# Landed keys copied by ScalarE, three raw-weight buffers, and a new hand-written order: a gated linear recurrence followed by a PReLU network on one core

## The chip, the cores and the metric

The kernel runs on one core of one Trainium2 chip. The metric is the device time of one execution in microseconds, lower is better. Five engines work in parallel, each through its own instructions in program order: TensorE (PE; its weight loads are listed as PEld), VectorE (DVE), ScalarE (ACT), GpSimd (POOL) and SyncE (SP), which here only issues DMAs. An instruction that has to wait holds up everything behind it on its engine.

## The reference

Inputs are float32. The first part is a recurrence with a per-channel forget gate, the second a two-layer network on its output.

```python
batch, n_heads, seq, head_dim = (4, 8, 768, 48)
f = 1.0 / (1.0 + np.exp(-f_logit))
for t in range(S):
    state = f[:, :, t, :, None] * state + np.einsum('bhd,bhe->bhde', k[:, :, t], v[:, :, t])
    y[:, :, t] = np.einsum('bhd,bhde->bhe', q[:, :, t], state)
...
n_tokens, d_model, d_ff = (3072, 384, 2048)
x = y.transpose(0, 2, 1, 3).reshape(B * S, H * D)
h = x @ w_in
g = np.maximum(h, 0.0) + alpha * np.minimum(h, 0.0)
return (g @ w_out).astype(np.float32)
```

## The kernel before

The sequence is cut into 6 chunks of 128 positions and the batch into 2 pairs; one pair of one chunk is a step, so there are 12 steps, numbered 0 to 11, named `bp_c` (pair, chunk). The recurrence of a step is worked out as block products; its state is carried in the tiles `vs0` and `vs1`, one for each pair. The network of step n runs while the attention of step n+1 is worked out.

Each stage of a step is a Python generator, cut by `yield` into pieces:

- `P` (`prepare`, 8 pieces): load f, q, k, v (line 279, 288); sigmoid and copies on ScalarE (293 to 296); products on VectorE (307 to 313); scans (340, 341); two further pieces of VectorE products (347 to 357; `k4`, `us`); the keys scaled to the end of the block and, from the second chunk on, transposed by VectorE into `kt` (407 to 415); the queries `q3` (401, 440); ScalarE copies of them into the score tile `A` (453).
- `K` (`keys_moved`): 16 DMAs from `kt` to `ksn`, 8 issued by SP and 8 by GpSimd (463).
- `S`, `T` (`scores` for the two batches of a pair, 4 pieces each): products on PE (569, on the raw keys, then on `k4`), each followed by predicated copies into `ad` on VectorE (578, 588, 604).
- `O` (`carry`): products between halves of a chunk (497), their ScalarE copies into `A` (504), the state increments on PE (532) and the state update `moved(0)` on VectorE (542, 546). In chunk 0 the keys go through PE transposes and ScalarE copies (514, 518) and not through DMAs. In later chunks two small products with an identity (525) read one column of each landed block of `ksn` just before the state increments; all waits for the 16 DMAs stand on these two.
- `Y` (`attend`): `ad` copied into `A` (612), the output products (623), the copy `y` (630), `moved(1)`, and the DMAs that lay `y` out as `xT` (653); in step 0 this layout is done by PE (642, 644).
- `n` (`network`, 13 pieces after step 0): 8 blocks `ph` of hidden units (668), each followed by a ScalarE pass `neg` (673) and two VectorE passes `gate` (675), sums of gates (754), then 7 products of the second layer, `pa` to `pe` (707), with sums on VectorE (711) and stores from SP (683). The products share four PSUM banks in turn. In step 0 the second layer is the plain one, `po` (688).
- `a`, `w` (w_in, 8 pieces each) and `b`, `g` (w_out): a raw piece of weights of 768 KB is loaded by SP (229), ScalarE splits it with two passes (233, 234), VectorE adds the halves (243). The raw pieces go through `RAWS` buffers in turn. `W` derives the sums of w_out (773), `i` is one idle product that writes nothing used (779), `X` hands over PSUM banks.

The order in which PE, VectorE, ScalarE and SP get their instructions is written out by hand: `START` lists pieces up to step 4, `USUAL` is the pattern for every later step, in which a bare letter means step n, `+` means step n+1, and `n` means the network of step n-1. `S:2` means two pieces of S. The words before are in the diff below. GpSimd's own order follows from its program order and is nearly untouched.

Of the kernel before, what the change touches and what calls it, by code (L numbers as in the profile page):

```python
# [21 lines left out]
U = 2  # L22
# [1 line left out]
NC2 = C // CH  # L24
NB = DB // 4
WP = 768
RAWS, LEADS = 5, 4
UP = 2.0 ** 16

BEGUN = 5  # L30
START = (
# [7 lines left out]
)  # L39
USUAL = "S:2 T:2 n:3 P+ n S P+ T S n:3 T n Y n O P+ O P+ O Y n O P+ Y:2 n:2 P+:2 K+ n P+"  # L40

LOOSE = ("a", "w", "b", "g", "W", "i", "X")

def flat(start, usual, steps=12):
    out = []
    for word in start.split():
        key, _, times = word.partition(":")
        out += [(key,) if key in LOOSE else (key[0], int(key[1:]))] * int(times or 1)
    for n in range(BEGUN, steps + 1):
        for word in usual.split():  # L50
            key, _, times = word.partition(":")
            m = n + key.count("+") - (key == "n")
            if m < steps:
                out += [(key[0], m)] * int(times or 1)
    return out

ORDER = flat(START, USUAL)


@with_exitstack  # L60
def kernel(
# [30 lines left out]
    nc = tc.nc  # L92
# [3 lines left out]
    D = DM // H  # L96
# [3 lines left out]
    T = U * C  # L100
    W = U * HP * C
# [70 lines left out]
    for m in range(1, NB):  # L172
        lo = UO[m] + (4 if m == 1 else 0)
        n = NB - m
# [4 lines left out]
    for half in range(2):  # L179
        for m in range(1, NQ):  # L180
            n = NQ - m
# [9 lines left out]
    ident = const.tile([128, 128], F32, tag="ident", name="ident")  # L191
# [65 lines left out]
    def rows(par):  # L257
        return slice(64 * par, 64 * par + D)
# [4 lines left out]
    def halves(cc):  # L263

        return slice(CH * cc, CH * cc + CH), slice(CH * (1 - cc), CH * (1 - cc) + D)
# [191 lines left out]
    def keys_moved(bp, c, x):  # L457
# [7 lines left out]
                    in_=kt[32 * a:32 * (a + 1)].rearrange("p (g b x) -> p g b x", b=NJ, x=32)[:, :, b, 0:n])  # L465
        yield

    def carry(bp, c, x):

        i = f"{bp}_{c}"  # L470
        home = more if (bp, c) == steps[0] else pairs
        off = home[0]
        if not c:
            half = home[1]
            for u in range(U):
                for hp in range(HP):
                    for j in range(NJ):
                        g = (u * HP + hp) * NJ + j
                        o = (u * HP + hp) * 16
                        for par in range(2):  # L480
                            r_ = rows(par)
                            nc.tensor.matmul(half[DB * j:DB * (j + 1), par, o:o + 16], lhsT=x["k16"][r_, g],
                                             rhs=x["q16"][r_, g], start=True, stop=True)
            yield
            for u in range(U):
                o = u * HP * 16
                nc.scalar.copy(ad[:, u, :, :, 16:DB], half[:, :, o:o + HP * 16].rearrange("p r (h t) -> p r h t", h=HP))  # L487
            yield
        q3, ks, kh, f64 = (x[n] for n in ("q3", "ks", "kh", "f64"))
        for u in range(U):  # L490
            for hp in range(HP):
                a = (u * HP + hp) * NC2
                h_ = slice(64 * (hp % 2), 64 * (hp % 2) + 2 * DB)
                o = (u * HP + hp) // 2 * 2 * DB
                for par in range(2):
                    r_ = rows(par)
                    nc.tensor.matmul(off[h_, par, o:o + 2 * DB], lhsT=kh[r_, a:a + 2].rearrange("p c s -> p (c s)"),  # L497
                                     rhs=q3[r_, a:a + 2, 2], start=True, stop=True)
        yield
        for cc in range(NC2):  # L500
            s_ = slice(CH * cc, CH * cc + DB)
            for e in range(2):
                of = off[64 * e + DB * cc:64 * e + DB * (cc + 1), :, 0:U * HP * DB]
                nc.scalar.copy(A[s_].rearrange("p u (r h e) t -> p r u h e t", r=2, e=2)[:, :, :, :, e, CH * cc + DB:CH * (cc + 1)],
                               of.rearrange("p r (u h c t) -> p r u h c t", u=U, h=HP // 2, c=NC2)[:, :, :, :, cc])


        if not c:
            yield
            pk = home[1]  # L510
            for u in range(U):
                for hp in range(HP):
                    a = (u * HP + hp) * NC2
                    nc.tensor.transpose(pk[:, u, hp * 128:(hp + 1) * 128], ks[:, a:a + 2].rearrange("p c s t -> p (c s t)"), ident)
            yield
            ksn = x["ksn"] = work.tile([128, U, HP * 128], F32, tag="ksn", name=f"ksn_{i}", bufs=1)
            for u in range(U):
                nc.scalar.copy(ksn[:, u], pk[:, u])
        yield
        pd = home[1]  # L520
        ksn = x["ksn"]
        if c:
            for par in range(2):
                r_ = slice(64 * par, 64 * par + 64)
                nc.tensor.matmul(pd[r_, par, 508:512], lhsT=ident[r_, r_], rhs=ksn[r_, 0, 0:128:32], start=True, stop=True)  # L525
        for u in range(U):
            for hp in range(HP):
                for cc in range(NC2):
                    for par in range(2):
                        o = (u * HP + hp) * D  # L530
                        s_ = halves(cc)[0]
                        nc.tensor.matmul(pd[rows(par), cc, o:o + D],  # L532
                                         lhsT=ksn[s_, u, hp * 128 + 64 * par:hp * 128 + 64 * par + D],
                                         rhs=vs[bp][s_, cc, u, (2 * hp + par) * D:(2 * hp + par + 1) * D], start=True, stop=True)

        def moved(cc):

            of, to = halves(cc)[1], halves(1 - cc)[1]
            was, then = (vs[bp][p, a, :, 0:DM].rearrange("p u (h e) -> p u h e", e=D)
                         for p, a in ((of, cc), (to, 1 - cc)))  # L540
            if c or cc:
                nc.vector.tensor_tensor(then, was, f64[of].unsqueeze(3).broadcast_to((D, U, H, D)), ALU.mult)
            for par in range(2):
                now = pd[rows(par), cc, 0:U * HP * D].rearrange("p (u h e) -> p u h e", u=U, e=D)
                if c or cc:
                    nc.vector.tensor_tensor(then[:, :, par:H:2], then[:, :, par:H:2], now, ALU.add)
                else:
                    nc.scalar.copy(then[:, :, par:H:2], now)

        x["moved"] = moved  # L550
        yield
        moved(0)
        yield
# [236 lines left out]
    with tc.manual_schedule(engines={mybir.EngineType.PE, mybir.EngineType.DVE, mybir.EngineType.Activation,  # L790
                                     mybir.EngineType.SP}):
        run = {}
        for n, step in enumerate(steps):
            x = {}
            for key, stage_ in zip("POYKn", (prepare, carry, attend, keys_moved, network)):
                run[key, n] = stage_(*step, x)
            run["S", n], run["T", n] = (scores(u, *step, x) for u in range(U))
        for key in ORDER:
            next(run[key] if key in run else pieces[key[0]])
# [55 lines left out]
```

## Time and profile before

| what | value |
|---|---|
| median of 3 runs | 609.65 us (608.31 to 610.66) |
| profiled execution: time | 608.89 us |
| profiled execution: span in the trace | 607.1 us |
| granted TensorE clock, mean | 0.994 |
| PE busy | 583.9 us, 96% |
| VectorE busy | 495.0 us, 82% |
| ScalarE busy | 242.3 us, 40% |
| GpSimd busy | 85.4 us, 14% |
| DMA | 50.36 MB, mean 83 GB/s |

The span runs from the first to the last instruction of the trace; 1.79 us of the execution's time lie around it. PE's busy time is modelled from pipelined products, so a busy PE can still have small gaps between groups. Times inside the trace are counted from the start of the span. A wait is put down to the engine that released it; "issue" is a stretch in which an engine waited for nothing that the trace shows.

### The profile page before, as it was taken

The numbers are of one execution on the slowest core, as the hardware profiler recorded it, in microseconds if no ns is written. First come the engines' busy times: TensorE is split into PE (matmuls) and PEld (weight loads), VectorE is DVE, ScalarE is ACT, GpSimd is POOL, SyncE is SP. The second block draws the span as 40 slices with busy tenths as digits, with TensorE's granted clock in tenths as the row PEclk, the third lists the DMA queues.
The fourth block names the chain that finished last, engine by engine and source line by source line (L and its number), as shares of the span: only waits on it lengthen the run. The fifth ranks groups of instructions, "written<-read, shape, count | busy, mean of one in ns | idle before, by whom it ended". The sixth has DMA issues, their size and how long they took to land.

```text
span 607.1 us, 18178 instructions
## 1 busy us (share of the span) xinstructions
PE 583.9 (96%) x7786; PEld 521.8 (86%) x7786; DVE 495.0 (82%) x998; ACT 242.3 (40%) x419; POOL 85.4 (14%) x162
## 2 busy tenths in 40 slices
PE   4679999999999999999999999999999999999997
PEld 2568767899899899899899899899889899899997
DVE  7889999998997788598888988988988986982351
ACT  4579944424513712341550541542433424322110
POOL 9210014023003003003001201200300300300000
PEclk9979999999999999999999999999999999999999
DMA  8949516123033111402501601601601601201000
GB/s 269 312 148 350 186 37 141 36 77 92 11 94 99 19 27 36 149 2 56 155 2 46 165 3 42 169 3 41 171 1 39 170 4 29 53 2 24 30 1 26
DMA packets 52880, 50.36 MB, mean 83 GB/s; under 512 B 26720, under 2 KB 43360, under 8 KB 52800
## 3 DMA queue, kind: packets, MB, share of 16 engines
q1 hardware_dynamic: 42784, 37.46, 21.2%
q0 software_dynamic: 5504, 9.90, 6.4%
q10 hardware_dynamic: 4512, 1.85, 1.3%
q8 instruction: 61, 1.00, 0.7%
q14 instruction: 19, 0.16, 0.1%
HBM read 36.21 MB, written 4.72 MB: 67 GB/s over the span
## 4 chain that ended last, share of the span: by engine, by line
PE 92%; ACT 1%; issue 1%; DMA 1%; SPq 0%; DVE 0%; ACTq 0%; DVEq 0%
PE ph L668 42%; PE pa L707 10%; PE pc L707 9%; PE pair L569 6%; PE pe L707 5%; PE pd L707 4%; PE pb L707 4%; PE pair L623 4%; PE po L688 3%; PE pair L532 1%; PE pair L497 1%; DMA xT<-y 1%; PE pair L525 1%; PE xt L642 0%; ACT us L334 0%
## 5 line engine op out<-in xcount | busy, mean ns | idle before, releaser
L668 PE MATMUL ph<-xT,w_in_sb 128*128 128x256 f32 x1152 | 255.7, 381 | 0.0
L668 PEld LDWEIGHTS ph<-xT,w_in_sb 128*128 128x128 f32 x1152 | 216.7, 190 | 31.5 <-issue 1.4
L675 DVE SCALAR_TENSOR_TENSOR gate<-neg,om,ph 128x256 f32<-128x256 f32 x192 | 81.9, 479 | 40.0 <-ACT neg L673 39.8
L673 ACT ACTIVATE neg<-ph 128x512 f32<-128x512 f32 x96 | 56.3, 595 | 115.6 <-PE ph L668 76.9
L707 PE MATMUL pa<-w_out_sb,gate 128*128 128x192 f32 x352 | 61.9, 329 | 0.0
L707 PE MATMUL pc<-t,S 128*128 128x192 f32 x352 | 61.6, 328 | 0.0
L707 PEld LDWEIGHTS pa<-w_out_sb,gate 128*128 128x128 f32 x352 | 57.5, 190 | 1.3
L707 PEld LDWEIGHTS pc<-t,S 128*128 128x128 f32 x352 | 57.4, 190 | 0.4
L453 ACT COPY A<-q 48x512 f32<-48x512 f32 x44 | 27.1, 616 | 74.8 <-DVE q L401 74.4
L463 POOL DMA_DIRECT2D ksn<-kt x80 | 46.2, 586 | 73.2 <-DVE kt L415 46.6
L653 POOL DMA_DIRECT2D xT<-y x22 | 11.9, 545 | 302.5 <-ACT y L630 302.4
L588 DVE COPY_PREDICATED ad<-mquad,pair 128x224 f32<-128x224 int32 (+6 forms) x140 | 41.7, 298 | 5.8 <-PE pair L569 1.7
L578 DVE COPY_PREDICATED ad<-mraw,pair 128x256 f32<-128x256 int32 (+1 forms) x96 | 41.1, 452 | 4.3 <-ACT ad L487 1.3
L711 DVE SCALAR_TENSOR_TENSOR Csum<-pc,Csum 128x192 f32<-128x192 f32 x22 | 7.8, 356 | 39.9 <-PE pc L707 39.8
L357 DVE TENSOR_TENSOR us<-us,fs 128x768 f32<-128x768 f32 (+5 forms) x60 | 36.9, 615 | 1.1
L612 ACT COPY A<-ad 32x512 f32<-32x512 f32 x48 | 29.5, 615 | 20.4 <-DVE ad L588 19.8
L754 DVE TENSOR_TENSOR S<-gate 128x512 f32<-128x512 f32 x44 | 30.3, 688 | 0.8
L707 PE MATMUL pe<-w_out_sb,S 128*128 128x192 f32 x176 | 30.5, 327 | 0.0
L707 PE MATMUL pb<-t,gate 128*128 128x192 f32 x176 | 30.4, 326 | 0.0
L707 PE MATMUL pd<-w_out_sb,S 128*128 128x192 f32 x176 | 30.4, 326 | 0.0
L630 ACT COPY y<-pair 128x512 f32<-128x512 f32 x22 | 11.8, 589 | 46.4 <-PE pair L623 45.8
L707 PEld LDWEIGHTS pe<-w_out_sb,S 128*128 128x128 f32 x176 | 28.9, 190 | 0.1
(121 smaller groups left out, 740.6 us busy)
## 6 DMA issues: line engine op xcount, KB each, us to landing
w_out_raw<-in_w_out SPq DMA_DIRECT2D x8, 767.8 KB, 7.2
w_in_raw<-in_w_in SPq DMA_DIRECT2D x8, 767.2 KB, 10.4
out<-o SPq DMA_DIRECT2D x23, 192.0 KB, 2.0
q<-in_qT SPq DMA_DIRECT2D x8, 512.0 KB, 4.7
k<-in_kT SPq DMA_DIRECT2D x8, 512.0 KB, 5.9
f<-in_fT SPq DMA_DIRECT2D x7, 512.0 KB, 3.9
vs<-in_v SPq DMA_DIRECT2D x16, 192.0 KB, 6.4
ksn<-kt SPq DMA_DIRECT2D x80, 32.0 KB, 2.1
```

Source lines behind the costliest of these rows:

```text
L357: nc.vector.tensor_tensor(us[:, :, UO[m]:UO[m] + 4 * n].rearrange("p g (i r) -> p g i r", r=4), us[:, :, skip:skip + 4 * n].rearrange("p g ...
L453: nc.scalar.copy(A[halves(cc)[1], :, par * HP:(par + 1) * HP, CH * cc:CH * (cc + 1)], q3[rows(par)].rearrange("p (u h c) s t -> p u h c (s ...
L463: (nc.gpsimd if a % 2 else nc.sync).dma_start(out=ksn[32 * b:32 * (b + 1)].rearrange("p u (h x) -> p (u h) x", h=HP)[:, :, 32 * a:32 * a + n],
L569: nc.tensor.matmul(to[DB * j:DB * (j + 1), par, hp * step + lo:hp * step + hi], lhsT=keys[r_, g * DB:(g + 1) * DB], rhs=by[r_, g, lo:hi], ...
L578: nc.vector.copy_predicated(adu[:, :, :, d:4], mraw[:, d, :, d:4].bitcast(I32).unsqueeze(1).broadcast_to((128, H, NB, n)), rv[:, :, QO[d]: ...
L588: nc.vector.copy_predicated(ad[:, u, :, :, 4 * m:DB], mquad[:, lo:lo + n].bitcast(I32).unsqueeze(1).unsqueeze(1).broadcast_to((128, 2, HP, ...
L612: nc.scalar.copy(A[s_].rearrange("p u h t -> p (u h) t")[:, :, s_], ad[s_].rearrange("p u r h t -> p (u r h) t"))
L668: nc.tensor.matmul(ph[:, j * T:(j + 1) * T], lhsT=w_in_sb[:, kt, m * 128:(m + 1) * 128], rhs=xT[:, kt], start=(kt == 0 and j == 0), stop=( ...
L673: nc.scalar.activation(neg, phv, AF.Relu, scale=-1.0)
L675: nc.vector.scalar_tensor_tensor(gate[:, m % NH, m // NH], neg[:, j], om[:, m:m + 1], phv[:, j], ALU.mult, ALU.add)
L707: nc.tensor.matmul(to[:, 0:DH], lhsT=of(f), rhs=by(f), start=(f == 0 and not more), stop=(f == NH - 1), skip_group_check=True)
L754: nc.vector.tensor_tensor(to, x_, y_, op)
```

## The change

Three things change.

1. The two identity products of line 525 go. A new stage `M` (`landed`) takes their place: one ScalarE instruction copies the 48 used columns of each block of `ksn` back into the tile `kt`, and the state increments read `kt`. The wait for the 16 DMAs stands on this copy.
2. `RAWS` goes from 5 to 3.
3. `START` and `USUAL` are replaced. `START` now begins with the first piece of w_in (load, split, add), ahead of the loads of step 0. In `USUAL`, `K` moves to the end of the step, behind the last store of the network; `M` stands behind the fifth network piece; the four pieces of `O` stand together.

Lines of the code after `keys_moved` are numbered 7 higher in the changed kernel up to line 519, and 3 higher from line 526 on.

```diff
-RAWS, LEADS = 5, 4
+RAWS, LEADS = 3, 4
 START = (
-    "i P0:3 S0 i P0:2 T0 i O0:2 a i P0:2 P1 i T0 i:3 O0 T0 O0 P1 S0 P1 S0 O0 T0 S0 i w P0 i P1 O0 P1 O0 i "
-    "Y0:2 O0 a S1 Y0 O1 Y0 O1 X a S1 w Y0 T1 P2 T1 w a:2 w P1 n0 a:2 P1 w a w S1 P2 S1 n0 T1 w P1 w b "
...
+    "a i w P0:3 S0 P0:2 O0 a O0 i:2 P0:2 i T0 a S0 T0 i O0 P0 P1:2 S0 T0 S0 P1 O0 T0 w O0 a i:2 O0 P1 i:2 "
+    "Y0 O0 i:2 S1 Y0 O0 P1 Y0:2 w O1:2 a S1 X Y0 a T1 P2 w T1 n0 w S1 w P1 T1 a P2 S1 a P1 n0 T1 b n0:2 "
...
-USUAL = "S:2 T:2 n:3 P+ n S P+ T S n:3 T n Y n O P+ O P+ O Y n O P+ Y:2 n:2 P+:2 K+ n P+"
+USUAL = "S T S T n:4 P+ M n T S T P+ S P+ n:2 Y n Y O:4 n:2 Y P+:2 Y n:2 P+:2 n P+ K+"
...
+    def landed(bp, c, x):
+        parts = "p u (g x) -> p (u g) x"
+        kn = x["kt"].rearrange("p (u y) -> p u y", u=U)
+        nc.scalar.copy(kn.rearrange(parts, x=64)[:, :, 0:D], x["ksn"].rearrange(parts, x=64)[:, :, 0:D])
+        x["ksn"] = kn
+        yield
...
-        if c:
-            for par in range(2):
-                r_ = slice(64 * par, 64 * par + 64)
-                nc.tensor.matmul(pd[r_, par, 508:512], lhsT=ident[r_, r_], rhs=ksn[r_, 0, 0:128:32], start=True, stop=True)
...
-            for key, stage_ in zip("POYKn", (prepare, carry, attend, keys_moved, network)):
+            for key, stage_ in zip("POYKMn", (prepare, carry, attend, keys_moved, landed, network)):
```

10 rows, old and new, of the table START are left out of this document.

## The prediction

> **What bounds the kernel now.** I read the busy totals, the slices and the chain's shares first. The two rows marked PE are its share in the totals and its busy tenths in 40 slices; the last line is the chain that ended last.
>
> ```profile
> PE 583.9 (96%) x7786; PEld 521.8 (86%) x7786; DVE 495.0 (82%) x998; ACT 242.3 (40%) x419; POOL 85.4 (14%) x162
> ...
> PE   4679999999999999999999999999999999999997
> ...
> PE 92%; ACT 1%; issue 1%; DMA 1%; SPq 0%; DVE 0%; ACTq 0%; DVEq 0%
> ```
>
> From slice 4 on (45 us) PE never stops; the table of windows gives it 46.92 us of the 47.12 us of a late step. So the time is: when PE's unbroken run begins (first network block, 45.16 us), plus PE's own work, plus any wait that the new order puts into it. Second, the chain in order of time (start, length, what) round the two products that go:
>
> ```profile
> 403.46 2.60 PE pb L707 x16
> 406.06 0.62 PE pair L497 x32
> 406.85 0.20 issue
> 407.05 0.19 PE pair L525
> 407.24 0.81 PE pair L532 x62
> 408.05 2.80 PE pc L707 x16
> ```
>
> L497 ends at 406.68, L532 begins at 407.24: line 525 with its waits costs PE 0.56 us. Third, the timeline of the start, rows of ScalarE and PE:
>
> ```profile
> 1.68 1.28 ACT L293 ACT_TABLE_LOAD   x1 [1.68 <-PEq L847]
> ...
> 4.43 0.63 ACT L293 ACTIVATE f<-f 128x512 f32<-128x512 f32 x1 [0.15 <-DMA f<-in_fT]
> ...
> 19.89 0.90 ACT L234 ACTIVATE w_in_sb<-w_in_raw 128x768 int32<-128x768 uint32 x1
> ...
> 27.96 1.25 ACT L453 COPY A<-q 48x512 f32<-48x512 f32 x2
> ...
> 31.49 1.07 ACT L518 COPY ksn<-more 128x512 f32<-128x512 f32 x2
> ...
> 36.50 2.09 PE L623 MATMUL more<-A,vs 128*64 128x64 f32 x64
> ```
>
> The sigmoid waits for f, then ScalarE runs without a gap from 23.8 to 37.7 us, and PE waits 5 us for L518.
>
> **Line 525 gone.** The chain shows the gap of 0.56 us in eight of the ten steps that have it, and 0.21 us in two (126.35 to 126.57, 158.50 to 158.71), where L525 follows longer blocks. 8 x 0.56 + 2 x 0.21 = 4.9 us off PE, if L532 finds its keys ready. All PE products from the first network block on are otherwise the same set in another order.
>
> **The copy M.** No row has 128x768 float32 on ScalarE as a copy; L234 writes 128x768 in 0.91 us, L453 48x512 in 0.62, L296 128x1024 in 1.05. I take 0.85, and 0.3 for sixteen semaphores (17 ns apiece in the waits of L463), 1.15 us in all. ScalarE is 40% busy, so its time is hidden; what counts is when it may run and who stands behind it. In a late step, from the start of the raw-key products (376.43 in the trace) as zero:
>
> ```profile
> 378.04 5.37 SPq L463 DMA_DIRECT2D ksn<-kt  x8
> ...
> 383.23 0.36 DVE L711 SCALAR_TENSOR_TENSOR o<-pe,o 128x192 f32<-128x192 f32 x1
> ...
> 383.66 0.40 SPq L683 DMA_DIRECT2D out<-o  x1
> ...
> 388.62 0.60 ACT L673 ACTIVATE neg<-ph 128x512 f32<-128x512 f32 x1 [0.19 <-PE ph L668]
> 389.24 1.06 ACT L293 ACTIVATE f<-f 128x1024 f32<-128x1024 f32 x1
> ```
>
> K now stands behind that store on SP, so its eight issues run from 7.6 to 13.0 and not from 1.6; the last lands 2.0 us (median of L463) after its issue at 12.4, at about 14.5 to 15.0. The fourth `neg` ends at 12.7, M ends near 16.2, the fifth `neg` (block ready at 14.7) near 16.8. Behind it on VectorE: fifth gate to 17.65, both predicated copies (2 x 2.2) to 22.0, the seven products from L307 on (3.6, now ahead of gates 5 to 7) to 25.7, gates to 28.1; `pa` begins at 25.9 on PE and wants the last gate's first half after 2.4 us, at 28.3; that half is done at 27.7. So PE does not wait, with 0.5 us to spare. Also queued behind K: the loads of f, q, k and v, 384.10 before and some 5 us later now. f lands near 17.5 (3.9 us, median), the sigmoid follows, and its user L307 comes at 22. Hidden. The same walk for the bank of the fifth block (gate 0 done at 11.3, wanted at 12.1) leaves 0.8 us.
>
> **The start.** Raw piece 0 goes ahead of f on SP. 767 KB at the 314 to 335 GB/s of the windows from 2 to 6 us are 2.3 us; f lands at 6.1 and 6.9, not 3.6 and 4.4. ScalarE splits the piece first (5.3 to 7.0: 1.7 from 19.09 to 20.79). The changed program holds a second table load between this and the sigmoid: 1.28 by the row, to 8.3. The second half's sigmoid starts at 8.95, 4.5 us late. The Trainium skill (ScalarE: Activation LUTs, "What ACT_TABLE_LOAD costs") counts a switch at 2.66 us, with a drain of 1.38 beside the load; the trace's one load agrees on 1.28 and shows no drain, since ScalarE waited for f there. By the page the sum below would be 1.4 us higher.
>
> Of the 4.5 us, 1.5 vanish in the wait of VectorE for GpSimd (12.2 to 13.68); `q3` is done at 23.3 and not 20.4. From there ScalarE's work up to the output products, by the trace's start-to-start times: L453 1.28, L293 to L296 2.60, L504 1.52, one raw piece 1.75, L518 0.96, L334 and L336 2.25, L612 2.53, L548 0.96, 13.85 in all: 37.15. Before, the output products began at 36.57. Gone from this stretch are PE's ten idle products at 18.6 to 23.0, which L497 had waited behind, and one raw split. So the first network block begins 0.6 us later, 45.8. Bounds: if nothing were hidden, the whole 4.5; if the ScalarE chain started with `q3` as early as before, -2.3.
>
> **Three buffers.** Piece n may load when n-3 is split, not n-5. By ScalarE's new order raw splits end at 7, 16, 22, 30, 44, 47, 51, 55 us and for w_out from 57.5 to 83.4; each load (7.2 us median) is issued three splits ahead and lands before its turn, the tightest (last piece: issued 73.8, turn at 81.6) by 0.6 us. PE wants its last piece at 93. Hidden.
>
> **The new order between 45 and 235 us.** VectorE is busy 14.5 of 15 us in these windows, so order matters. Walking its new list with the durations above: `q3` of step 1 is done at 57.5 (PE wants it at 58.3), the last gate of the next network at 122.0 (124.0), `moved(0)` of step 2 at 126.5 (the output products, now right behind `pb`, want it at 126.9). No wait, but 0.4 to 2 us to spare where my walk may be 1 us off. Bounds: 0 to 3 us; I take 0, the side on which all three fall.
>
> **Sum.** 608.89 us + 0.6 - 4.9 = 604.6. That execution lies 0.76 under the median of the runs; I put half of this back: 605.0.
>
> **Rivals.**
> 1. *The copy comes late, slower.* M waits for the last of 128-byte pieces, and ScalarE, then VectorE, then `pa` wait behind it. For: only 0.5 us to spare, K now 6 us later, and L463 landings up to 4.8 us. Against: the long landings need heavy traffic, and the loads come behind K in the queue. It decides when the last landing takes over 2.5 us. At 4.0, PE waits 1.5 us in each of eight steps: 605.0 + 12 = 617; at 3.2, 610.6. I put it at 614.
> 2. *The start eats the gain.* f, the table switch and the ScalarE chain hide nothing: first network block 4.5 us later, 609. For: ScalarE has no gap from 23.8 to 37.7. Against: 1.5 us of VectorE's wait are certain cover.
> 3. *The change does not do what it says on PE.* The 0.56 us are not the waits but the turn from one kind of product to another, and L532 pays them anyway, or VectorE's ties take them: 608.5 to 609.5. For: 0.2 of it is "issue". Against: at 76.2 us L532 follows L569 without a gap.
>
> **How the numbers follow.** Forecast 0.55, rival 1 0.15, rival 2 0.17, rival 3 0.13. About 0.5% (3.05 us) is what a measurement can tell from no change: under 606.6 is faster, over 612.7 slower. The forecast gives 0.52 of faster (its own range 602.3 to 607), rivals 2 and 3 another 0.04; they and the upper edge of the forecast give 0.28 of same; rival 1 most of slower. The range 602.3 to 612 leaves out 0.05 below (ScalarE's chain earlier) and 0.12 above.
>
> **What would show it.** In the profile of the changed kernel: two table loads, the second near 7 us, and the first L293 near 8.3; the output products of step 0 (L623 before) near 37.2; the first `ph` at 45.8; late steps 46.56 us long, L532's rows 0.0 us behind L497's; `M` ending before the fifth `neg` is 2.5 us old; no wait of `pa` for a gate. Wrong it is if a late step is 47.1 or longer, or the first `ph` is later than 48.

## The result, and the profile after

The changed kernel takes 614.35 us (611.93 to 631.0, 8 runs), the kernel before 609.63 us (8 runs): the ratio is 1.0073, 95% interval 1.0048 to 1.0098. The forecast was 605.0 with a range up to 612.0; the change makes the kernel about 4.5 us slower. The first profile of the changed kernel caught a disturbed execution (631.0 us), so the one read here is a later one, of 613.87 us with a span of 612.1 (`e1` below).

The busy totals, PE's slices and the chain's shares of the changed kernel:

```profile
PE 582.0 (95%) x7746; PEld 519.7 (85%) x7746; DVE 494.6 (81%) x998; ACT 248.2 (41%) x430; POOL 80.4 (13%) x162
...
PE   0598999999999989999999999999999999999997
...
PE 59%; DVE 2%; issue 0%; DVEq 0%
```

PE still bounds the kernel, with 2 us less work. (The chain of this profile can be followed back only to 235 us, so its 59% stands for PE in the last 61% of the span.) PE's slices are 15.3 us each. The first has fallen from 4 to 0 and the second from 6 to 5, the third has risen from 7 to 9, and two new places stand under 9: the fourth (46 to 61 us, where the first network block now starts) and the fifteenth (214 to 230 us). The late steps are not among them. Here is the chain of the changed kernel round the place of the two products that went (start, length, what):

```profile
408.80 0.62 PE pair L504 x32
409.42 0.72 PE pair L535 x64
410.14 2.80 PE pa L710 x16
```

L504 (L497 before) ends at 409.42 and L535 (L532 before) begins at 409.42. The gap of 0.56 us is gone, and a late step takes 46.39 us (L535 of one step starts at 362.85 in PE's timeline, which shows products that overlap a little earlier than the chain does, and that of the next at 409.24), against 47.12.

The start is where the time went. The timeline of ScalarE in the changed kernel (start, length, line, operation; in brackets what it waited for):

```profile
1.65 1.28 ACT L233 ACT_TABLE_LOAD   x1 [1.65 <-PEq L850]
7.00 0.88 ACT L233 ACTIVATE w_in_lead<-w_in_raw 128x768 f16<-128x768 bf16 x1 [4.07 <-DMA w_in_raw<-in_w_in]
...
8.69 1.28 ACT L293 ACT_TABLE_LOAD   x1
9.98 1.15 ACT L293 ACTIVATE f<-f 128x512 f32<-128x512 f32 x2
...
28.47 1.06 ACT L293 ACTIVATE f<-f 128x1024 f32<-128x1024 f32 x1 [2.14 <-DMA f<-in_fT]
...
32.07 1.49 ACT L511 COPY A<-more 32x256 f32<-32x256 f32 x4 [0.92 <-PE more L504]
...
36.50 1.07 ACT L525 COPY ksn<-more 128x512 f32<-128x512 f32 x2 [1.21 <-PE more L521]
```

The same line before, and ScalarE's one wait in this stretch before:

```profile
3.64 0.63 ACT L293 ACTIVATE f<-f 128x512 f32<-128x512 f32 x1 [0.68 <-DMA f<-in_fT]
...
23.84 1.49 ACT L504 COPY A<-more 32x256 f32<-32x256 f32 x4 [3.05 <-PE more L497]
```

The first sigmoid starts at 9.98 us (3.64 before). After `q3`, ScalarE before waited once, 3.05 us for the products of L497, and then ran without a gap up to the output products. Now it waits three times: for f of step 1, for L504, and for L521. PE's timeline of the changed kernel in the same stretch tells why:

```profile
23.93 0.75 PE L572 MATMUL pair<-qd,k 48*32 48x80 f32 x22
28.76 1.03 PE L572 MATMUL pair<-qd,k 48*32 48x80 f32 x42 [4.07 <-issue]
...
34.50 1.97 PE L521 MATMUL more<-ident,ks 128*128 128x128 f32 x8
...
43.09 1.97 PE L626 MATMUL more<-A,vs 128*64 128x64 f32 x60 [0.76 <-ACT vs L551]
...
47.95 0.41 PE L489 MATMUL pair<-us 48*32 48x16 f32 x34 [1.98 <-issue]
48.28 4.54 PE L645 MATMUL xt<-y,dense 128*128 128x256 f32 x12
...
53.60 2.64 PE L671 MATMUL ph<-xT,w_in_sb 128*128 128x256 f32 x11
```

And before:

```profile
25.63 1.09 PE L514 MATMUL more<-ident,ks 128*128 128x128 f32 x8
...
41.12 0.41 PE L482 MATMUL pair<-us 48*32 48x16 f32 x34 [1.63 <-issue]
41.45 2.86 PE L642 MATMUL xt<-y,dense 128*128 128x256 f32 x12
...
45.09 2.86 PE L668 MATMUL ph<-xT,w_in_sb 128*128 128x256 f32 x12
```

In the middle of one group of products PE stands still for 4.07 us and waits for nothing that the trace shows. After that L521 takes 1.97 us (1.09 before) and `xt` 4.54 (2.86): the granted clock in the table of windows is 0.50 from 30 to 38 and from 50 to 52 us. The output products come at 43.09 (36.50 before), the first network block at 53.60 (45.09).

The other new place is in step 4 (PE's timeline, then ScalarE's, of the changed kernel):

```profile
213.31 0.94 PE L535 MATMUL pair<-vs,kt 64*48 64x48 f32 x64 [0.47 <-ACT kt L471]
...
224.38 0.59 PE L710 MATMUL pa<-w_out_sb,gate 128*128 128x192 f32 x2 [0.19 <-DVE gate L678]
226.47 0.59 PE L710 MATMUL pa<-w_out_sb,gate 128*128 128x192 f32 x2 [1.49 <-DVE gate L678]
...
246.57 13.22 PE L671 MATMUL ph<-xT,w_in_sb 128*128 128x256 f32 x60 [0.17 <-DVE Csum L714]
```

```profile
202.50 0.60 ACT L676 ACTIVATE neg<-ph 128x512 f32<-128x512 f32 x1 [1.99 <-PE ph L671]
212.43 0.83 ACT L471 COPY kt<-ksn 128x768 f32<-128x768 f32 x1 [9.33 <-DMA ksn<-kt]
213.17 1.08 ACT L676 ACTIVATE neg<-ph 128x512 f32<-128x512 f32 x2
```

ScalarE stands 9.33 us in the copy of step 4, because SP issues that step's `K` only from 204.86 on, behind a store, and the copy stands right behind it. The next two `neg` passes (L676) queue behind the copy, VectorE's gates come late, and `pa` waits. PE loses 0.47 + 0.19 + 1.49 + 0.17 = 2.3 us.

So the account of the two profiled executions is: start +8.5 us (45.09 to 53.60); all that follows −3.5 us (span minus first block: 562.0 before, 558.5 after), which is +2.3 in step 4 and, as the remainder, −5.8 saved; in sum +5.0, from 608.89 to 613.87.

### The profile page after: what moved, and what is told of

It reads as the page before. It is cut to its first block, busy times and chain, and to the rows that moved or that the text cites. A ratio compares the mean times of both kernels' runs of the same rounds, so it can differ in the third digit from the quotient of the medians.

```text
span 629.2 us, 18037 instructions
## 1 busy us (share of the span) xinstructions
PE 600.4 (95%) x7746; PEld 530.4 (84%) x7746; DVE 494.9 (79%) x998; ACT 249.4 (40%) x430; POOL 80.4 (13%) x162
## 4 chain that ended last, share of the span: by engine, by line
PE 91%; DVE 3%; ACT 2%; issue 2%; DMA 1%; SPq 1%; ACTq 0%; DVEq 0%
PE ph L671 39%; PE pa L710 10%; PE pc L710 9%; PE pair L572 6%; PE pe L710 5%; PE pd L710 5%; PE pb L710 5%; PE pair L626 4%; PE po L691 4%; PE pair L535 1%; PE pair L504 1%; DMA w_in_raw<-in_w_in 1%; PE xt L645 1%; SPq L463 1%; PE more L782 1%
## 5 line engine op out<-in xcount | busy, mean ns | idle before, releaser
L671 PE MATMUL ph<-xT,w_in_sb 128*128 128x256 f32 x1152 | 265.3, 392 | 0.0
L671 PEld LDWEIGHTS ph<-xT,w_in_sb 128*128 128x128 f32 x1152 | 220.0, 193 | 38.0 <-issue 1.5
L676 ACT ACTIVATE neg<-ph 128x512 f32<-128x512 f32 x96 | 56.2, 595 | 123.0 <-PE ph L671 95.2
L710 PE MATMUL pa<-w_out_sb,gate 128*128 128x192 f32 x352 | 64.9, 339 | 1.1 <-DVE gate L678 1.1
L710 PE MATMUL pc<-t,S 128*128 128x192 f32 x352 | 63.2, 335 | 0.0
L710 PEld LDWEIGHTS pc<-t,S 128*128 128x128 f32 x352 | 59.8, 192 | 0.1
L572 PE MATMUL pair<-qd,k 48*32 48x80 f32 x1536 | 21.2, 244 | 15.5 <-ACT us L334 11.9
L572 PEld LDWEIGHTS pair<-qd,k 48*32 48x32 f32 x1536 | 17.9, 109 | 20.9 <-ACT us L334 12.6
L710 PE MATMUL pe<-w_out_sb,S 128*128 128x192 f32 x176 | 31.8, 336 | 0.0
```

The source lines that it names most:

```text
L572: nc.tensor.matmul(to[DB * j:DB * (j + 1), par, hp * step + lo:hp * step + hi], lhsT=keys[r_, g * DB:(g + 1) * DB], rhs=by[r_, g, lo:hi], ...
L671: nc.tensor.matmul(ph[:, j * T:(j + 1) * T], lhsT=w_in_sb[:, kt, m * 128:(m + 1) * 128], rhs=xT[:, kt], start=(kt == 0 and j == 0), stop=( ...
L676: nc.scalar.activation(neg, phv, AF.Relu, scale=-1.0)
L710: nc.tensor.matmul(to[:, 0:DH], lhsT=of(f), rhs=by(f), start=(f == 0 and not more), stop=(f == NH - 1), skip_group_check=True)
```

## The experiments

Each kernel was run beside the kernel before on the same chip; times are medians, with the ratio to the kernel before. Lines of `e5` and `e6` stand 3 higher from the places of their edits on.

**The changed kernel again, the copy alone, the sigmoid first, five buffers** (one chip; before 609.86).

> The changed kernel once more, for a profile. Theory A (the start costs, PE's saving is real): time 614, first network block at 53 to 54.5 us against 45.2 before, a late step 46.6 us against 47.1. Theory B (the three buffers hold the weights back): first network block near 46, and PE waits for weights after it. Theory C (the copy comes late): first block near 46, a late step 47.5 us, with waits of PE for gates.

Measured: 613.91 us, ratio 1.0066 (1.0045 to 1.0086). First block at 53.6, late step 46.39: theory A on both counts. No product of PE waits for weights after the first block, against B; the waits for gates are in step 4 alone, so C holds for one step.

`e2_copy_alone`, the order and buffers of before and the new stage (L525 gone, `RAWS` 5):

```diff
-n1:3 T3 S3:2 n1 T3 n1:2 O2:2
+n1:3 T3 S3:2 n1 M2 T3 n1:2 O2:2
-K3 Y3 n2:3 O3
+K3 Y3 n2:2 M3 n2 O3
-K4 Y4 O4:3
+K4 Y4 M4 O4:3
-USUAL = "S:2 T:2 n:3 P+ n S P+ T S ...
+USUAL = "S:2 T:2 n:3 P+ n M S P+ T S ...
```

> The order and the five buffers of before, with the copy in place of the two products with their waits. A: start as before (first network block 45.2), late steps 46.6, so 604.7 (609.6 less 4.9). C, or that the products' 0.56 us are paid anyway: 609 or more, late steps 47.1 or longer.

Measured: 607.58 us, 0.9973 (0.9956 to 0.9990), between the two. The late step is 46.50 us, so PE's saving is real (0.62 a step). Two losses took the rest in its profile (an execution of 608.96): in step 4 L535 waited 2.23 us for the copy, which stood behind other copies on ScalarE, and the first block came at 46.77, 1.7 us later than in the profile of before, all of it in `xt` (4.53 us for 2.86) at half clock after a stall.

`e3_sigmoid_first`, the changed kernel with this edit in `START`:

```diff
-a i w P0:3 S0 P0:2 O0 a O0 i:2 P0:2 i T0 a S0 T0 i O0
+i P0:3 S0 P0:2 O0 a:2 O0 i:2 P0:2 i T0 a S0 T0 w i O0
```

> The changed kernel, with the first raw piece behind the first loads and the first sigmoid again. A: one table load, sigmoid near 3.7 us, first network block 46 to 48, time 606 to 608. B or C: the first block moves as in A, if at all, but the time stays above 611.

Measured: 607.90 us, 0.9969 (0.9949 to 0.9989). One table load, sigmoid at 3.79, first block at 46.60: 6.0 us under `e1` with the order of one piece. The same kernel on another chip (`e16` below) had a ratio of 0.9991, which is 4.6 us under `e1`'s, so the piece is worth 4.6 to 6.0.

`e4_five_buffers`: `RAWS` 5 in the changed kernel, nothing else.

> The changed kernel with five raw buffers. A: 613 to 615, first network block within 1 us of the changed kernel's. B: 609 or less, first block 3 us or more earlier than the changed kernel's.

Measured: 614.92 us, 1.0083 (1.0052 to 1.0115), first block at 53.41. Theory B falls for the changed order.

**What in the first piece costs, step 4, and the start of before** (one chip; before 609.90).

`e5_one_table`, the changed kernel with, ahead of everything on ScalarE:

```diff
+    tiny = const.tile([128, 1], F32, tag="tiny", name="tiny")
+    nc.vector.memset(tiny, 0.0)
+    nc.scalar.activation(tiny, tiny, AF.Sigmoid)
```

> The changed kernel with a sigmoid of one column ahead of everything on ScalarE, so that its table is there before the raw piece lands. D1 (what delays the start is f's transfer behind the raw piece's; the second table load is 1.3 us of it): first sigmoid at 8.7 us, not 9.98, first network block 52.3 to 53.6, time 612.6 to 613.9. D2 (the table switch is the main price): first block 3 us or more earlier than 53.6, time 611 or less.

Measured: 611.25 us, 1.0033 (1.0005 to 1.0061). There is one table load and the sigmoid starts at 8.66, 1.3 us earlier, as D1 has it; but the time fell by 2.7 and the first block came 4.3 us earlier (49.33). The stalls of PE in its start were 2.70 and 0.97 us here (4.07 and 0.42 in `e1`), and `xt` ran at full clock: what follows the sigmoid is not a fixed distance from it. Neither theory held in all its numbers, and with ten runs from 609.59 to 615.24 the price of the second load alone stays open.

`e6_load_first`, the kernel of `e3` with the raw piece's DMA alone ahead:

```diff
-i P0:3 S0 P0:2 O0 a:2
+a i P0:3 S0 P0:2 O0 a:2
...
             nc.sync.dma_start(out=raw...
+            if name == "w_in" and not n:
+                yield
             lead = stage.tile(...
...
-                upper(n)
+                yield from upper(n)
```

> The kernel with the sigmoid first again (607.9), except that the raw piece's transfer alone is issued ahead of f's; its split stays behind the sigmoid, so there is one table load. D1: sigmoid at 7.8 to 8.5 us, first network block 50 to 53, time 611 to 613.5. D2: sigmoid at 4 to 6 us, first block 46.6 to 48, time 608 to 609.

Measured: 611.48 us, 1.0031 (1.0014 to 1.0048); first block at 52.38. ScalarE's timeline of this kernel:

```profile
1.64 1.28 ACT L296 ACT_TABLE_LOAD   x1 [1.64 <-PEq L853]
7.76 1.30 ACT L296 ACTIVATE f<-f 128x512 f32<-128x512 f32 x2 [4.84 <-DMA f<-in_fT]
```

ScalarE was free from 2.9 us on, and f landed at 7.8. D1 holds: the transfer alone brings most of the delay. Against `e3` it costs 3.6 us (611.48 to 607.90) and leaves 2.4 of the 6.0 for the split and the second table load; against `e16` it costs 2.5, so the shares are known to about 1 us.

`e7_mended`, the kernel of `e3` with step 4's copy and raw-key products later:

```diff
-T4 S4 M4 n3:2 Y4 P5 n3 O4:2 P5 O4 n3:2
+T4 S4 n3:2 Y4 P5 n3 O4:2 P5 M4 n3 O4 n3
```

> The kernel with the sigmoid first again (607.9), and in step 4 the copy and the raw-key products behind it moved some blocks of the network later. If the waits of 0.5, 1.7 and 0.2 us there (raw-key products on the copy, pa on gates, a block on the sum) come from ScalarE standing in the copy: they go, 605.6. If they come from VectorE's new order: they stay, 607.9.

Measured: 607.40 us, 0.9957 (0.9940 to 0.9974). The waits of `pa` and of the block are gone, as they should be if ScalarE standing in the copy made them. But L535 now waited 1.31 us, since the copy stood behind the copies into `A` (L511).

`e8_start_of_before`: before's `START` with `M2` and `M3` as in `e2` and `K4 Y4 O4:2 M4 n3 O4 P5:2 O4 n3:2`, five buffers, the changed `USUAL`.

> The start of before (five buffers) with the copy in it, one block of room before step 4's raw-key products, and the late steps in the changed order. If start and late order are independent: first block 45.1 to 46.8 as before and with the copy alone, late steps 46.4, time 602 to 605. If the two halves don't fit (waits where they join, in steps 4 to 6): 606 or more.

Measured: 608.39 us, 0.9974 (0.9961 to 0.9988). First block at 45.55, late steps 46.39, and in step 4 waits of 0.94 us (L535 for the copy) and 2.08 (output products for `vs`, as the products were now a block later). The time lies in the range of the second alternative, but the trace puts the waits on my place for the copy and not on the join; the next run tries this.

**The copy of step 4 earlier, a warmer PE, one buffer** (one chip; before 609.74).

`e9_copy_early_step4`, the kernel of `e8` with the copy a block of the network earlier, and the products where they were:

```diff
-n3:2 P5 n3:3 K4 Y4 O4:2 M4 n3 O4 P5:2 O4 n3:2
+n3:2 P5 n3:2 K4 M4 n3 Y4 O4:3 P5:2 O4 n3:3
```

> As the kernel with the start of before and the changed late order (608.4), but in step 4 the moves and the copy stand one block of the network earlier and the raw-key products where they were. If its waits of 0.9 and 2.1 us in step 4 come from where the copy stands: both go, with the half clock after them (1.2): 604 to 605, first network block 45.1 to 46.8. If the join of the two orders makes them: 607 or more.

Measured: 604.53 us, 0.9916 (0.9893 to 0.9938): the best kernel of all, 5.2 us under before. PE has no wait over 0.1 us after the first block. That block came at 48.17 in the profiled execution (45.1 to 46.8 was expected), the slowest of the four runs (606.19; the others 603.43 to 604.67).

`e10_mended_more`, the kernel of `e7` with the copy ahead of the copies into `A`: `T4 S4 n3:2 Y4 P5 M4 n3 O4:2 P5 n3 O4 n3`.

> As the mended kernel (607.4), with step 4's copy ahead of the A copies on ScalarE. The wait of 1.3 us of the raw-key products goes, no other wait of PE after the first network block over 0.2 us: 606; the first block at 46.5 to 49.2, as it varied between the two profiles of this start. If the landing, not ScalarE's order, sets that wait: 607.4.

Measured: 607.31 us, 0.9955 (0.9937 to 0.9973). No wait after the first block any more, as expected, but the first block came at 49.92 (46.5 to 49.2 was expected), so the time stayed and the 606 was missed.

`e11_kept_warm`, the kernel of `e10` with `i:5` for `i:2` ahead of the first `Y0`.

> The same with three more idle products ahead of the first output products, where PE waited 1.6 to 1.8 us for ScalarE and its clock then fell to half. If the clock costs: the output products take 2.1 us, not 2.5 to 3.4, no half clock at 38 to 41 us, first block 0.4 to 1.3 us earlier than the kernel beside it: 605. If the chain of ScalarE alone sets the first block: the same time within 0.3 us.

Measured: 609.23 us, 0.9974 (0.9953 to 0.9994). A miss: the wait ahead of the output products is gone, but the idle products made them begin 1.1 us later (39.27, in `e10` 38.12) and end 0.6 later, the stall of 2.3 us behind them came all the same, and `xt` ran at half clock in both. First block 50.47. The wait was 0.65 us in this profile of `e10` and left the clock at 1.00, so the case that was to be tried did not occur; filling the wait bought nothing.

`e12_one_buffer`, the changed kernel with `RAWS` 1, one run; PE waits for weights later, so the time (641.7) says nothing.

> The changed kernel with a single raw buffer, so that few raw pieces are on the way while PE's instructions and the loads of step 1 are fetched; PE waits for weights later, so only the profile up to 45 us counts. If traffic makes those late (theory D): f of step 1 landed by 25 us, not 28.4, the stall of PE in the first step's products 2 us or less, not 4.1, output products at 40 us or before, not 43.1. If not: the same to 1 us.

Measured: DMA issues of `e1` and then of `e12` between 17 and 19 us (KB each, us from issue to landing):

```profile
f<-in_fT POOLq DMA_DIRECT2D x1, 512.0 KB, 10.7
```

```profile
f<-in_fT POOLq DMA_DIRECT2D x1, 512.0 KB, 4.2
```

f of step 1 was issued at the same time and landed at 22, not at 28.4; the stall of PE was 2.71 us, not 4.07; the main output products came at 40.79, not 43.09, which misses the 40 that were expected. So the traffic of the raw pieces holds f back. What that costs the run does not say: f's sigmoid began at 28.29 all the same (28.47 in `e1`), because ScalarE stood 3.83 us for a raw piece ahead of it. For the stall the evidence is weaker: it missed the 2 us that were expected, and in kernels with the changed order it ranged from 1.2 to 4.1 us.

**What still lay between `e9` and the changed kernel** (one chip; before 609.61).

`e13_three_buffers`: `RAWS` 3 in the kernel of `e9`.

> The kernel of 604.5 (start of before, copy, changed late order) with three raw buffers in place of five. If the buffers are hidden, as forecast: 604 to 605.5, no wait of PE for weights. If they are part of what the changed start costs: 606 or more, with waits of PE for weights between 45 and 93 us.

Measured: 607.66 us, 0.9968 (0.9957 to 0.9978), intervals apart from `e9`. ScalarE's and PE's timelines:

```profile
54.24 0.91 ACT L233 ACTIVATE w_in_lead<-w_in_raw 128x768 f16<-128x768 bf16 x1 [2.11 <-DMA w_in_raw<-in_w_in]
...
67.20 1.09 PE L521 MATMUL pair<-ident,ks 128*128 128x128 f32 x8 [1.60 <-DVE ad L607]
```

A split waits for its piece, and then all of ScalarE and VectorE behind it. In the order of the start of before three buffers cost about 3 us; in the changed order five gained nothing (`e4`).

`e14_raw_first`: the kernel of `e9` with the first piece ahead of everything.

```diff
-i P0:3 S0 i P0:2 T0 i O0:2 a i P0:2
+a i w P0:3 S0 i P0:2 T0 i O0:2 i P0:2
```

> The kernel of 604.5 with one edit: the first raw piece's load, split and rest ahead of everything, as in the changed kernel. If that edit alone is the price of the start (6.0 by two runs before): two table loads, first sigmoid near 10 us, 609.5 to 611.5. If it was the rest of the changed start: 605 to 607.

Measured: 610.20 us, 1.0011 (1.0001 to 1.0021), 5.7 us over `e9` with one edit. The second table load stands at 8.83, the sigmoid at 10.13 and the first block at 51.54.

`e15_mended_again` and `e16_sigmoid_first_again`: the kernels of `e10` and `e3` once more.

> The changed order with the sigmoid first and step 4 mended, beside the next one on the same chip. If the waits of step 4 are worth what the traces say (2.2 us): 605.5 to 606.5, 1.5 to 2.6 under the next one. If something takes it back: within 0.7 of it.

> The changed order with the sigmoid first and step 4 as changed: 607 to 609, as before.

Measured: 607.33 us (0.9953, 0.9934 to 0.9972) and 609.01 us (0.9991, 0.9972 to 1.0010), 1.7 us apart on one chip, inside the 1.5 to 2.6 that were expected, though both times lie above the forecast ones: step 4's waits are worth about what the trace says, less the spread of the start, which was 49.92 and 48.91 in these two.

The steps from `e9` (604.5) to the changed kernel (613.9) are thus three. `e10` has the changed order of the start with its three buffers, but the sigmoid first and step 4 mended; it is 2.8 us slower than `e9` on the same chip, and no run took these 2.8 apart. Step 4's copy is 1.7 (2.3 by the trace). The raw piece ahead of the sigmoid is 4.6 to 6.0.

The first block's place, one profile for each kernel, falls into three groups, each over 2 us wide: 45.1 to 48.2 with the order of the start of before (`before`, `e2`, `e8`, `e9`, `e13`), 46.6 to 49.9 with the changed order and the sigmoid first (`e3`, `e7`, `e10`, `e15`, `e16`), and 51.5 to 53.6 with the raw piece, its split and the second table load first (`e1`, `e4`, `e14`). The first two overlap; the third stands apart.

## Why the prediction was wrong, point by point

**Line 525 gone (−4.9): right.** The gap went whole, L535 has its keys, and rival 3's turn from one kind of product to another costs nothing that the trace shows. A late step is 46.39 us and not 46.56; what was saved after the first block is 5.8 us, the remainder of the account above. In the kernel of `e2`, with the order of before, the step is 46.50, so 0.62 of the 0.73 a step is line 525 and 0.11 the new order.

**The copy (1.15 us, hidden, done at 16.2): right in the late steps.** It takes 0.83 us. In the late step whose raw-key products begin at 384.29, ScalarE's timeline has:

```profile
399.66 0.84 ACT L471 COPY kt<-ksn 128x768 f32<-128x768 f32 x1 [2.52 <-DMA ksn<-kt]
400.40 0.59 ACT L676 ACTIVATE neg<-ph 128x512 f32<-128x512 f32 x1
402.15 1.06 ACT L293 ACTIVATE f<-f 128x1024 f32<-128x1024 f32 x1 [1.16 <-DMA f<-in_fT]
```

The copy ends at 400.5, 16.2 us after that zero, the fifth `neg` ends at 16.7 (forecast near 16.8) and f's sigmoid at 17.9 (17.5). The last gate ends at 28.1 and `pa` begins at 25.8, as walked, and does not wait. Rival 1 did not come about in the late steps.

**The new order between 45 and 235 us (0, bounds 0 to 3): the bound held and the value did not.** Step 4 lost 2.3 us. The walk followed VectorE's list in three places and not ScalarE's queue at the copy of step 4. There `START` has `K4 T4 S4 M4`, with no network block between `K` and the copy, where `USUAL` has four (its `M` stands behind the fourth network piece, not the fifth). It is rival 1's chain of waits, in one step, and with `K` issued late as its cause and not a slow landing.

**The start (+0.6): this step failed, and with it the sign.** Rival 2, put at 0.17, had the place right and the size wrong (4.5 us; it measured 8.5), and its reason only in part: the cover of 1.5 us held. In the terms of the forecast, `q3` late by 2.9, a ScalarE list shorter by 2.3, and nothing more, became `q3` late by 4.6, the list shorter by 2.3, 4.2 of new waits in it, and 1.9 behind the output products; this is 8.4. Four pieces of the working failed:

- "f lands at 6.1 and 6.9": both halves took 6.3 us from issue (1.49 and some 0.5 later), so they landed near 7.8 and 8.3. The rate of 314 to 335 GB/s was that of other transfers, from 2 to 6 us of the old kernel; the changed one moved 0.11 MB in its first 3 us and 0.41 MB in its first 4 (0.30 and 0.66 before). The raw piece itself landed at 7.0, not 5.3.
- So the sigmoid came 6.3 us late, not 4.7. VectorE's wait for GpSimd did hide 1.5 as said (L380 4.6 us late at 18.27), and `q3` was done at 25.0, not 23.3.
- "13.85 in all" for ScalarE up to the output products was a sum of durations without waits. It took 18.0 us (25.09 to 43.09), the difference being the three waits shown above: 2.14 for f of step 1, 0.92 for L504 behind PE's stall, and 1.21 for L521 at half clock; they add up to 4.3, about the whole of it.
- The stretch from output products to first block was taken as 8.65, as before; it took 10.5, for a longer stall and `xt` at half clock (4.54 against 2.86).

The upper bound, "if nothing were hidden, the whole 4.5", was no bound: a later start met other transfers and a colder PE, and both added waits that the profile of before did not have.

The second table load took 1.28 us and the sigmoid began 0.01 us after it (8.69 + 1.28 = 9.97, started at 9.98). The Trainium skill (ScalarE: Activation LUTs, "What ACT_TABLE_LOAD costs") counts 1.38 us of drain more for a switch. No drain shows on ScalarE here, neither ahead of the load (the split ends at 8.67) nor behind it, and none was hidden under a wait this time; that the time fell by 2.7 us without the second load (`e5`) is more than this load, and other waits went with it.

**Three buffers (0): right for the changed order**, by `e4`; with the start of before they cost 3.1 us (`e13`). The walk took 7.2 us for every load, the median of the w_out pieces; the profile of before has 10.4 for those of w_in, and it is a w_in piece that the split waits for in `e13`.

**The sum:** 608.89 − 5.8 + 8.5 + 2.3 = 613.9, which closes by construction, as the 5.8 is the remainder.

## What to carry to other kernels

A transfer moved to the head of a queue delays what stands behind it: here f landed 4 us later, where a rate borrowed from other transfers gave 2.5. Read the rate for the start from the first microseconds of a trace, which moved 0.11 to 0.30 MB in 3 us here, and not from later ones. When a start is moved, add up waits and not durations: each engine's list has to be walked against what else will be on the way at the new time, and "nothing hidden" is no upper bound. Judge the parts of a bundled change one by one: here a saving of 5 us was there from the beginning, and the place of one piece in the order gave it back.

## What the runs showed of the hardware

**PE stalls at fixed places of its program.** The stalls that the trace calls "issue" stand behind the same number of products in every kernel where they occur, whichever products these are. Counted from the first product in PE's timeline:

```
products so far   222            350            732
before            L482, 1.87 us  L569, 0.39 us  L482, 1.63 us
e1                L572, 4.07     L572, 0.42     L489, 1.98
e3                L572, 1.23     L572, 2.34     no stall
```

`e11` has six more of these products ahead of the third place, through its three idle pieces, and its third stall stands behind the 88th product of L489 and not the 94th: again 732. The first stall ends 2 to 3 us after one packet of 16 KB on the queue called instruction appears. In `e1`, between 26 and 28 us, the queue's packets, MB and share are:

```profile
q8 instruction: 1, 0.02, 3.5%
```

The packet starts between 26.0 and 26.5 there, PE goes on at 28.76; before, between 15.5 and 16.0 and 18.05. At the third place it is the same: in `e1` a packet starts between 45.4 and 45.8 and PE goes on at 47.95, before between 38.6 and 38.8 and 41.12. This points to PE waiting for its own instructions, which arrive among the data; no run changed their transfer alone. The Trainium skill (Runtime: NRT & Kernel Launch, "Instruction fetch mechanics") has the sequencer fetch its program in blocks of 256 instructions, by DMA and ahead of use, at a cost that is mostly hidden. The 128 products from 222 to 350, with as many weight loads, are about one such block, and the 382 from 350 to 732 about three; that the cost is mostly hidden does not hold in these starts, where the stalls come to 3.9 us before and 6.5 in `e1`. What makes one fetch later than another was not separated.

**Short waits of PE lower its clock, or do not.** After a stall of 1.63 us before `xt` the granted clock stayed at 1.00 in the kernel before; after 2.03 us in `e2` it fell. The table of windows (PE, PEld, DVE, ACT, POOL busy, then the granted clock, DMA share, GB/s) has for the kernel before, and then for `e2`:

```profile
42.00:44.00 2.00, 2.00 (x11) 1.70 (x9) 1.90 (x5) 2.00 (x5) 0.00 (x0) 1.00 0.76 233
```

```profile
42.00:44.00 2.00, 2.00 (x7) 1.67 (x6) 1.90 (x5) 1.99 (x4) 0.00 (x0) 0.62 0.64 171
```

The same products took 2.86 and 4.53 us. In step 4 a wait of 1.49 us left the clock at 1.00 in `e1` and took it to 0.75 and 0.83 (221 to 229 us) in `e5`. The Trainium skill (TensorE: Matmul & The Clock Gate, "Part 1: The HAM clock gate") says that PE's activity is judged over a window that runs free of the kernel; that agrees with one wait of 1.49 us having both effects, though no run here shows the window itself. A wait of 1.5 to 2 us can so cost as much again, or nothing, and the start of one and the same kernel varied by 2.3 us: 46.60 and 48.91 to the first block in `e3` and `e16`, with other stalls and other stretches of half clock.
